# A fused attention, MoE and Fourier MLP kernel: TensorE and the load queue ordered by hand after attention

## The chip, the cores and the metric

The kernel runs on one core of a Trainium2 chip. The metric is the device time of one execution in microseconds (us), as the median of several runs. The engines are TensorE (PE in the rows; PEld is its weight load), VectorE (DVE), ScalarE (ACT), GpSimd (POOL) and SyncE (SP), which here only issues transfers.

## The reference

Three parts follow each other, on 4 batches of 544 tokens (512 local and 32 global ones) and 512 features.

1. Attention, 8 heads of 64: 32 global tokens attend to all, 512 local tokens attend to a band of 32 on each side and to the global tokens.
2. An MoE-like block: `h = relu(x @ w_in)` (512 to 1024), a 3-tap convolution along the tokens, `h * sigmoid(conv) @ w_out` back to 512.
3. A Fourier mixer and MLP: `u = x + real(fft(fft(x, tokens), features))`, normalisation of u over the features, then `u + relu(un @ w_ch1) @ w_ch2` with 2048 hidden features.

Weights arrive as float64 and are turned into float32 pairs (high and low part) on the chip; each product is three matmuls (low x high, high x low, high x high).

## The kernel before

**Attention and MoE** run together, in an order written out by hand for TensorE and the load queue (SyncE's), under `manual_schedule`: these two engines take their instructions in the order of the code, while a planner orders the others by priority. MoE goes in units u = 0 to 63: batch, half of the tokens, one of 8 blocks of hidden features. `m_g1(u)` is 12 matmuls into bank `g1`, `m_conv`, `m_tanh` and `m_gate` work on ScalarE and VectorE, and `m_g2(u - 3)` is 12 matmuls into the four banks `a0` to `a3`. When attention ends, units up to 54 have had `m_g1`; the loop from `ulast + 1` = 55 to 66 does the rest. MoE writes its result into `eo_t[b]`, three slots of the pool `up` (tag `u`) for batches 0 to 2 and one on the right side for batch 3.

**The DFT** of a batch is the generator `fft(b)`, 12 steps: a preparation on VectorE and ScalarE (L651 to L657); six first-stage pieces, for three token groups an a-piece of 8 matmuls (cosine table `c2`, and the one-row table `co`) and a b-piece of 6 (`s2`); five second-stage pieces of 9 (`c1`, `s1`). Each piece takes the next of the PSUM banks `s` and `t` in turn, and VectorE (with ScalarE) empties it. The last step stores u to `u_d[b]` in DRAM.

**The MLP** takes tokens in five chunks of 436, across batches. `load_uc(c)` reads a chunk back from `u_d` into a slot of `up`; `ln(c)` is a generator that normalises it: sums over features by matmuls with `ones` into bank `t` (mean) and `s` (variance), the centring pass L767 on VectorE, squares on ScalarE, the rest on GpSimd (chunk 0: VectorE). `cf` holds the centred chunk and keeps a slot of `up` until the end. The steps v go through `plan`, 80 pairs of chunk and hidden block: chunks 0 and 1 in two halves by turns, then 2, 3 and 4. `c_g1(v)` and `c_g2(v - 2)` are groups of 12 matmuls. The factor 1/sqrt(var) is applied when a chunk's sum is added to u.

**Weights of the MLP**: 12 blocks (`KEPT`) are unpacked during attention through the slots `r0`, `r1` and `o` of pool `stp` and parked in DRAM; `fetch_c` loads them, or raw blocks, when MoE's weight slots come free; `make_c` unpacks a raw block in two passes on ScalarE, one on GpSimd and three on VectorE (L172, L173, L202), plus ScalarE's cast. The last 16 blocks (`tail`) wait until the DFT's pool `fp` closes at step 7.

**After attention** nothing is ordered by hand. The planner places each instruction by its own forecast of when inputs are there and by the priorities of `PRIORITY`. In the order of the code, each MoE iteration has four DFT steps, first of batch 0, then (with `ln(0)` begun) of batches 1 and 2; batch 3's come two to a step in MLP steps 0 to 6; `load_uc(0)` follows the MoE loop; chunks 1 to 4 are loaded at steps 2, 25, 36 and 52.

Of the kernel before, what the change touches and what calls it, by code (L numbers as in the profile page):

```python
# [33 lines left out]
KEPT = [0, 16, 1, 17, 2, 18, 3, 19, 4, 5, 6, 7]  # L34
NT = 436
# [91 lines left out]
def fused_kernel(ctx: ExitStack, tc: tile.TileContext, d, out):  # L127
# [100 lines left out]
    right = ExitStack()  # L228
    ap1 = right.enter_context(tc.tile_pool(name="ap1", bufs=1, side="right"))
# [9 lines left out]
    stp = right.enter_context(tc.tile_pool(name="stp", bufs=1, side="right"))  # L239
# [8 lines left out]
    @prio("keep")  # L248
    def keep_load(x):
        if x is not None:  # L250
            w_raw[x] = fetch(stp, f"r{KEPT.index(x) % 2}", c_src(x))

    @prio("keep")
    def keep_make(x):
        if x is not None:
            packed[x] = put(stp, "o", unpack(mp, w_raw.pop(x), gp, True))
# [371 lines left out]
    last = ctx.enter_context(tc.tile_pool(name="last", bufs=1, side="right"))  # L628
    mag2 = last.tile([128, 512], F32, name="mag2")
# [3 lines left out]
    c2 = fp.tile([128, 2, 2, 258], F32R, name="c2")  # L633
    s2 = fp.tile([128, 2, 2, 256], F32R, name="s2")
    co = fp.tile([1, 258], F32R, name="co")
    c1 = fp.tile([92, 3, 2, NF], F32R, name="c1")
    s1 = fp.tile([92, 3, 2, NF], F32R, name="s1")
    u_t, u_d = {}, {}
# [79 lines left out]
    def c_slot(i):  # L718
        m = i % 16
        return (wp, f"w{m + (8 if i > 15 else 0)}") if m < 8 else (vp, f"v{i}")  # L720
# [16 lines left out]
    ln_t, uc_t = {}, {}  # L737
# [13 lines left out]
    def ln(c):  # L751
        n = width(c)
        ut = (uc_t[c] if c else u_t[0])[:, 0:4, 0:n]
        cf = cft[:, 0:4, 0:n]
# [8 lines left out]
        yield  # L763
        mu = bank("t")[:, 0:n]
# [12 lines left out]
        act.copy(sr[:, 0], cf[:, 0])  # L777
        dve.tensor_sub(sr[:, 1], cf[:, 0], f32(sr[:, 0]))
        yield
        yield  # L780
        va = bank("s")[:, 0:n]
        mm(va, ones, sr[:, 1], True, False)
        mm(va, ones, sr[:, 0], False, True)
        rs = uc_t[c][:, 4, 0:n]
        act.activation(rs, va, AF.Sqrt, bias=eps)
        dve.reciprocal(rs, rs)
        yield
# [22 lines left out]
    def c_g2(v):  # L810
# [15 lines left out]
        if m in last_:  # L826
            uc = uc_t[c]
            tmp = cft[:, 4, 0:n]
            for e in range(4):
                o = uc[:, e, 0:n]  # L830
                dve.tensor_mul(tmp, acc[e], uc[:, 4, 0:n])
                dve.tensor_add(o, o, tmp)
                if m == 15:
                    sp.dma_start(out[128 * e:128 * e + 128, NT * c:NT * c + n], o)

    for t, nm in ((c2, "c2"), (s2, "s2"), (c1, "c1"), (s1, "s1"), (co, "co")):
        gp.dma_start(t, d[nm])
    ffts = [fft(b) for b in range(4)]
    fq, lnq = ffts[0:1], []

    def step(queue, name):
# [7 lines left out]

    for u in range(ulast + 1, NM + LAG_G2):  # L850
        m_tanh(u - 1)
        m_g1(u, "g1")
        m_gate(u - 1)
        m_conv(u)
        m_g2(u - LAG_G2, 0)
        m_g2(u - LAG_G2, 1)
        for _ in range(4):
            step(fq, "fft")
        if not fq and not lnq:
            cft = up.tile([128, 5, NT], F32, tag="u", name="cf")  # L860
            lnq = [ln(0)]
            for _ in range(3):
                step(lnq, "ln0")
            fq = ffts[1:3]
# [5 lines left out]
    while fq:  # L870
        step(fq, "fft")
    left.close()
    lw = ctx.enter_context(tc.tile_pool(name="lw", bufs=1))
    mags += [mag2, lw.tile([128, 512], F32, name="mag1")]
    load_uc(0)
    while lnq:
        step(lnq, "ln")
    f3 = ffts[3:]
    vp = None
    tail = [x for m in range(8, 16) for x in (m, 16 + m)]  # L880
    for v in range(len(plan) + 2):
        if v < 7:
            step(f3, "f3")
            step(f3, "f3")
            if v < 4:
                make_c(20 + v)
        if v == 7:
            right.close()
            vp = ctx.enter_context(tc.tile_pool(name="vp", bufs=1, side="right"))
            for x in tail:  # L890
                fetch_c(x)
        if 8 <= v < 16:
            make_c(tail[2 * v - 16])
            make_c(tail[2 * v - 15])
# [49 lines left out]
```

## Time and profile before

| | us |
|---|---|
| median of 3 runs | 835.54 (834.47 to 838.54) |
| the profiled execution | 837.89 |
| its span, first to last instruction | 835.8 |
| TensorE busy in the span | 783.7 (94%) |
| VectorE busy | 484.1 (58%) |
| ScalarE busy | 364.0 (44%) |
| GpSimd busy | 170.0 (20%) |

The span is what the trace covers; the execution's own time has 2.1 us around it. Busy time is a sum over stages: attention fills roughly the first 334 us, MoE ends near 396, the DFTs near 477, and the MLP alone fills the rest. TensorE's granted clock is given beside the times as a share of 2.4 GHz; 0.5 is 1.2 GHz.

### The profile page before, as it was taken

Reading aid. Unit: us, or ns where it says so; the run is one execution under the profiler, and the core shown is the slowest. Engines: PE = TensorE matmul, PEld = TensorE weight load, DVE = VectorE, ACT = ScalarE, POOL = GpSimd, SP = SyncE. Lnnn points to the kernel's source line nnn. Section 1 sums busy time; section 2 is a strip of 40 time slices with the busy share of each in tenths; the row PEclk is TensorE's granted clock in tenths of the full one; section 3 lists DMA queues with packets and bytes.
Section 4 is the critical chain, followed back from the end, with each engine's and each line's share of the span. In section 5 each row is a group of like instructions: output and inputs, shape, how many; then the busy total and the mean of one; then the engine's idle time right before and its main releaser. Section 6 shows DMA issues by size and latency. Waiting matters only on the chain.

```text
span 835.8 us, 13613 instructions
## 1 busy us (share of the span) xinstructions
PE 783.7 (94%) x5272; PEld 715.1 (86%) x5272; DVE 484.1 (58%) x1162; ACT 364.0 (44%) x884; POOL 170.0 (20%) x219
## 2 busy tenths in 40 slices
PE   5769999999999999998998699999999999999996
PEld 3558888799889988997997589999999999999996
DVE  5898987668766876687726845853531232213112
ACT  5676787567666775546312156431222112111110
POOL 4544433223222321100000321111313003100000
PEclk9788999999999999999997699999999999999999
DMA  7743342344234420554022084002010011001001
GB/s 248 260 160 113 120 135 90 113 136 162 73 112 155 156 95 27 160 198 184 26 97 73 25 286 171 0 1 87 33 54 0 1 45 42 1 1 43 1 1 42
DMA packets 36896, 77.80 MB, mean 93 GB/s; under 512 B 3752, under 2 KB 22056, under 8 KB 36832
## 3 DMA queue, kind: packets, MB, share of 16 engines
q1 hardware_dynamic: 36000, 74.29, 26.0%
q0 software_dynamic: 832, 2.65, 1.3%
q8 instruction: 41, 0.67, 0.3%
q14 instruction: 23, 0.19, 0.1%
HBM read 62.11 MB, written 15.20 MB: 92 GB/s over the span
## 4 chain that ended last, share of the span: by engine, by line
PE 56%; DVE 15%; DMA 14%; ACT 10%; issue 2%; POOL 1%; SPq 1%; ACTq 0%; DVEq 0%; POOLq 0%
PE ps_a L144 25%; PE ps_g L144 14%; PE ps_pv L144 11%; DMA raw_r<-in_ch_dram 7%; PE ps_s L144 3%; ACT pb L319 3%; PE ps_t L144 2%; DMA raw_w<-in_w_in_dram 2%; DVE y L492 2%; DVE pb L307 2%; DVE y L493 2%; ACT mag L165 1%; DVE mag L173 1%; ACT y L499 1%; DMA co<-in_co_dram 1%
## 5 line engine op out<-in xcount | busy, mean ns | idle before, releaser
L144 PE MATMUL ps_g<-x,w_w 128*128 128x256 f32 (+1 forms) x768 | 113.4, 297 | 1.7 <-ACT h L481 1.7
L144 PE MATMUL ps_a<-g,w_w 128*128 128x254 f32 (+1 forms) x768 | 111.0, 292 | 0.0
L144 PEld LDWEIGHTS ps_g<-x,w_w 128*128 128x128 f32 x768 | 101.0, 190 | 11.3 <-issue 7.1
L330 POOL TENSOR_SCALAR pb<-pb,sm 128x224 f32<-128x224 f32 x128 | 82.8, 662 | 136.4 <-DVE sm L325 101.0
L144 PE MATMUL ps_a<-hd,w_w 128*128 128x436 f32 (+1 forms) x480 | 103.6, 361 | 1.2 <-ACT hd L806 1.2
L144 PEld LDWEIGHTS ps_a<-g,w_w 128*128 128x128 f32 x768 | 101.3, 189 | 0.5 <-issue 0.3
L144 PE MATMUL ps_a<-hd,w_v 128*128 128x436 f32 (+1 forms) x480 | 101.3, 361 | 0.0
L144 PEld LDWEIGHTS ps_a<-hd,w_w 128*128 128x128 f32 x480 | 89.6, 188 | 6.7 <-ACT hd L806 1.6
L144 PEld LDWEIGHTS ps_a<-hd,w_v 128*128 128x128 f32 x480 | 90.2, 188 | 5.1
L807 DVE SCALAR_TENSOR_TENSOR hd<-ps_g,hd 128x436 fp32r<-128x436 f32 (+1 forms) x40 | 24.2, 604 | 96.9 <-ACT hd L806 96.9
L807 DVE SCALAR_TENSOR_TENSOR hd<-ps_pv,hd 128x436 fp32r<-128x436 f32 (+1 forms) x40 | 24.4, 609 | 82.8 <-ACT hd L806 82.7
L166 POOL TENSOR_SCALAR mag<-mag 128x512 f32<-128x512 f32 x48 | 32.5, 678 | 181.6 <-ACT mag L165 181.1
L806 ACT ACTIVATE hd<-ps_pv 128x436 fp32r<-128x436 f32 (+1 forms) x40 | 21.3, 532 | 106.6 <-PE ps_pv L144 90.5
L806 ACT ACTIVATE hd<-ps_g 128x436 fp32r<-128x436 f32 (+1 forms) x40 | 21.3, 533 | 104.8 <-PE ps_g L144 81.6
L319 ACT ACTIVATE pb<-pb,sm 128x224 f32<-128x224 f32 x128 | 60.5, 475 | 12.9 <-DVE sm L307 12.9
L144 PE MATMUL ps_pv<-chl,w_w 128*128 128x436 f32 (+1 forms) x240 | 55.1, 377 | 6.9 <-POOL chl L769 3.5
L144 PEld LDWEIGHTS ps_pv<-chl,w_w 128*128 128x128 f32 x240 | 47.4, 199 | 10.9 <-POOL chl L769 3.8
L144 PE MATMUL ps_g<-chl,w_w 128*128 128x436 f32 (+1 forms) x240 | 52.1, 361 | 0.0
L144 PE MATMUL ps_pv<-chl,w_v 128*128 128x436 f32 (+1 forms) x240 | 50.9, 360 | 0.0
L144 PE MATMUL ps_g<-chl,w_v 128*128 128x436 f32 (+1 forms) x240 | 50.7, 360 | 0.0
L144 PE MATMUL ps_s<-qk 64*128 64x224 f32 (+1 forms) x144 | 37.5, 419 | 13.3 <-DMA qk<-in_qk_dram 4.2
L144 PEld LDWEIGHTS ps_g<-chl,w_w 128*128 128x128 f32 x240 | 44.9, 188 | 3.0 <-DVE hd L807 0.3
(203 smaller groups left out, 1397.2 us busy)
## 6 DMA issues: line engine op xcount, KB each, us to landing
v<-in_v_dram SPq DMA_DIRECT2D x16, 640.0 KB, 4.8
raw_v<-in_ch_dram SPq DMA_DIRECT2D x16, 512.0 KB, 10.8
qk<-in_qk_dram SPq DMA_DIRECT2D x16, 464.0 KB, 6.1
raw_r<-in_ch_dram SPq DMA_DIRECT2D x12, 512.0 KB, 6.4
kept<-w_o SPq DMA_DIRECT2D x12, 512.0 KB, 5.6
w_w<-kept SPq DMA_DIRECT2D x12, 512.0 KB, 3.3
qk<-in_qk_dram SPq DMA_DIRECT2D x16, 304.0 KB, 5.9
u_d<-u SPq DMA_DIRECT2D x4, 1088.0 KB, 6.4
```

Source lines behind the costliest of these rows:

```text
L144: return pe.matmul(o, a, b, start=start, stop=stop)
L165: act.activation(mag, f32(head), AF.Abs, scale=65536.0)
L166: (clamp or dve).tensor_scalar(mag, mag, TOP, 2.0, op0=ALU.min, op1=ALU.max)
L173: dve.scalar_tensor_tensor(val, head, -(2**31), val, op0=ALU.bitwise_and, op1=ALU.bitwise_or)
L307: anchor[i] = dve.tensor_tensor_reduce(out=pbs(i)[h][:, a, 0:224], in0=sb[h][:, a], in1=mask[:, 2 * where(i)[1] + a], scale=-0.125, scalar ...
L319: act.activation(p, p, AF.Exp, bias=sm[:, k:k + 1], scale=-1.0, accum_out=sm[:, 4 + k:5 + k])
L330: gp.tensor_scalar(p, p, sm[:, k:k + 1], 1.0, op0=ALU.mult, op1=ALU.mult)
L492: dve.scalar_tensor_tensor(y, hb[:, cc - 1:cc - 1 + n], convw2[:, m, 0:1], y, op0=ALU.mult, op1=ALU.add)
L493: dve.scalar_tensor_tensor(y, hb[:, cc + 1:cc + 1 + n], convw2[:, m, 2:3], y, op0=ALU.mult, op1=ALU.add)
L499: act.activation(g_t[u], g_t[u], AF.Tanh, scale=0.5)
L806: act.activation(hd[:, 0], o, AF.Relu)
L807: dve.scalar_tensor_tensor(hd[:, 1], o, 0.0, f32(hd[:, 0]), op0=ALU.max, op1=ALU.subtract)
```

## The change

From the end of attention on, TensorE and the load queue are ordered by hand as well (`manual_schedule` to the end of the kernel).

- All four DFTs form one list. `fstep` takes the next DFT step; right after the step that ends batch 1's DFT it writes chunk 1's load, after batch 2's chunk 0's load, and after batch 0's the first step of `ln(0)`. A MoE iteration has a DFT step ahead of `m_g1`, one ahead of `m_g2`'s first half, and in odd iterations one ahead of its second half: 30 of the 48 steps. MLP steps 0 to 5 have three each.
- `ln(0)` goes on in seven steps inside the MoE loop (two an iteration) and ends in MLP step 0; its 1/sqrt(var) gets a tile of its own, `rs0`. Chunk 1's `ln` begins at step 1, chunk 2's load moves from step 25 to 26, chunks 3 and 4 stay at 36 and 52. An `ln` advances by one generator step in each MLP step.
- The pool `rb` takes the place of `stp` and stays: `c2` and `s2` use the slots `r0` and `r1`, later three of the 16 late weight blocks use `r0`, `r1` and `o`. The tables are asked for in the order `c2`, `co`, `s2`, `c1`, `s1`, ahead of the other code of this stage.
- The late blocks load at step 8 in place of 7. Both `mag` buffers of the MLP lie in the pool `lw`.

```diff
+TAIL = [x for m in range(8, 16) for x in (m, 16 + m)]
...
+    rb = ctx.enter_context(tc.tile_pool(name="rb", bufs=1, side="right"))
...
-    stp = right.enter_context(tc.tile_pool(name="stp", bufs=1, side="right"))
...
-    last = ctx.enter_context(tc.tile_pool(name="last", bufs=1, side="right"))
-    mag2 = last.tile([128, 512], F32, name="mag2")
+    c2 = rb.tile([128, 2, 2, 258], F32R, tag="r0", name="c2")
+    s2 = rb.tile([128, 2, 2, 256], F32R, tag="r1", name="s2")
+    co = rb.tile([1, 258], F32R, name="co")
+    for t, nm in ((c2, "c2"), (co, "co"), (s2, "s2")):
+        gp.dma_start(t, d[nm])
...
+    for t, nm in ((c1, "c1"), (s1, "s1")):
+        gp.dma_start(t, d[nm])
+    ctx.enter_context(tc.manual_schedule(engines={mybir.EngineType.SP, mybir.EngineType.PE}))
...
-        return (wp, f"w{m + (8 if i > 15 else 0)}") if m < 8 else (vp, f"v{i}")
+        if m < 8:
+            return (wp, f"w{m + (8 if i > 15 else 0)}")
+        k = TAIL.index(i) - 13
+        return (vp, f"v{i}") if k < 0 else (rb, ("r0", "r1", "o")[k])
...
         yield
         yield
+        if c == 0:
+            yield
         mu = bank("t")[:, 0:n]
...
-        rs = uc_t[c][:, 4, 0:n]
+        rs = rs_t[c] = uc_t[c][:, 4, 0:n] if c else rs0
...
-    for t, nm in ((c2, "c2"), (s2, "s2"), (c1, "c1"), (s1, "s1"), (co, "co")):
-        gp.dma_start(t, d[nm])
-    ffts = [fft(b) for b in range(4)]
-    fq, lnq = ffts[0:1], []
+    fq = [fft(b) for b in range(4)]
+    lnq = []
...
+    def fstep(n=1):
+        for _ in range(n):
+            step(fq, "fft")
+            for c, b in ((1, 1), (0, 2)):
+                if b in u_d and c not in uc_t:
+                    load_uc(c)
+            if 0 in u_d and not lnq and not ln_t:
+                lnq.append(ln(0))
+                step(lnq)
+
+    early = 7
+
     for u in range(ulast + 1, NM + LAG_G2):
+        fstep()
         m_tanh(u - 1)
         m_g1(u, "g1")
         m_gate(u - 1)
         m_conv(u)
+        if lnq and early:
+            early -= 1
+            step(lnq)
+        fstep()
         m_g2(u - LAG_G2, 0)
+        if u % 2:
+            fstep()
         m_g2(u - LAG_G2, 1)
-        for _ in range(4):
-            step(fq, "fft")
...
+        if lnq and early:
+            early -= 1
+            step(lnq)
...
-    load_uc(0)
-    while lnq:
-        step(lnq, "ln")
-    f3 = ffts[3:]
...
     for v in range(len(plan) + 2):
-        if v < 7:
-            step(f3, "f3")
-            step(f3, "f3")
+        if v < 8:
+            for _ in range(3):
+                fstep()
             if v < 4:
                 make_c(20 + v)
-        if v == 7:
+        if v == 8:
+            while fq:
+                fstep()
             right.close()
...
+        while v == 0 and lnq:
+            step(lnq)
-        if v in (2, 25, 36, 52):
-            c = {2: 1, 25: 2, 36: 3, 52: 4}[v]
-            load_uc(c)
+        if v in (1, 26, 36, 52):
+            c = {1: 1, 26: 2, 36: 3, 52: 4}[v]
+            if c > 1:
+                load_uc(c)
             lnq.append(ln(c))
-        step(lnq, "ln")
+        step(lnq)
         c_g1(v)
         c_g2(v - 2)
```

## Rows read from the trace of the kernel before

**Rows 1.** The page, granted TensorE clock in 40 slices, tenths of full speed.
```profile
PEclk9788999999999999999997699999999999999999
```

**Rows 2.** Windows: stretch, length, busy PE, PEld, DVE, ACT, POOL (count), clock, DMA share, GB/s.
```profile
337.10:388.80 51.70, 48.48 (x362) 45.94 (x360) 37.98 (x78) 25.64 (x59) 1.06 (x3) 1.00 0.64 214
388.80:392.10 3.30, 2.80 (x8) 2.58 (x9) 3.21 (x7) 2.63 (x3) 0.00 (x0) 0.50 0.03 5
392.10:450.30 58.20, 56.97 (x334) 52.27 (x333) 30.47 (x61) 14.04 (x30) 2.32 (x3) 1.00 0.12 44
450.30:470.70 20.40, 17.58 (x70) 13.97 (x69) 15.97 (x25) 5.01 (x10) 3.40 (x2) 0.50 0.32 99
470.70:477.50 6.80, 5.24 (x33) 3.65 (x32) 6.15 (x12) 1.65 (x1) 0.87 (x1) 1.00 0.00 0
477.50:484.30 6.80, 3.62 (x10) 3.34 (x11) 4.34 (x2) 1.66 (x1) 5.03 (x2) 0.50 0.18 70
484.30:494.00 9.70, 8.46 (x42) 7.35 (x40) 1.88 (x4) 3.28 (x6) 1.87 (x3) 1.00 0.83 272
494.00:828.80 334.80, 334.80 (x1691) 317.22 (x1690) 119.57 (x174) 79.64 (x131) 41.89 (x30) 1.00 0.11 39
```

**Rows 3.** Waits of TensorE, 337 to 500 us: total, times, longest.
```profile
PE ps_pv L144 <- POOL chl L769: 3.5, 1, 3.5
```

**Rows 4.** Timeline of TensorE: start, length, instruction, tiles, count.
```profile
342.02 0.28 PE L144 MATMUL ps_t<-s,fl 128*92 128x256 f32 x1
...
342.73 1.77 PE L144 MATMUL ps_g<-x,w_w 128*128 128x292 f32 x12
...
349.89 0.28 PE L144 MATMUL ps_s<-c,fl 128*92 128x258 f32 x1
...
351.10 0.50 PE L144 MATMUL ps_a<-g,w_w 128*128 128x254 f32 x2
...
360.25 1.31 PE L144 MATMUL ps_s<-c,ab 92*128 92x274 f32 x9
...
503.23 2.55 PE L144 MATMUL ps_g<-chl,w_w 128*128 128x436 f32 x12
```

**Rows 5.** Timeline of VectorE: first and last pass preparing the first DFT.
```profile
334.25 0.72 DVE L651 TENSOR_TENSOR ff<-u 128x548 f32<-128x548 f32 x1
...
338.64 0.73 DVE L657 TENSOR_TENSOR fl<-ff,fh 128x548 fp32r<-128x548 f32 x1 [0.32 <-ACT fh L656]
```

**Rows 6.** Groups of VectorE's instructions by line, 374 to 530 us.
```profile
L786 DVE RECIPROCAL uc<-uc 128x436 f32<-128x436 f32 x2 | 5.8, 2876 | 1.5 <-ACT uc L785 1.5
...
L704 DVE TENSOR_TENSOR u<-u 128x544 f32<-128x544 f32 x6 | 4.3, 718 | 0.0
...
L202 DVE TENSOR_TENSOR w_w<-mag,w_w 128x512 fp32r<-128x512 f32 x4 | 2.7, 687 | 0.1
...
L767 DVE TENSOR_TENSOR cf<-u,ps_t 128x1744 f32<-128x1744 f32 x1 | 2.0, 1959 | 0.0
L689 DVE SCALAR_TENSOR_TENSOR u<-u,ps_t 128x273 f32<-128x273 f32 x4 | 1.8, 438 | 4.7 <-PE ps_t L144 4.7
```

**Rows 7.** Timelines of three engines between chunk 0's last group and chunk 2's mean.
```profile
567.45 5.36 PE L144 MATMUL ps_a<-hd,w_v 128*128 128x436 f32 x26
...
573.24 0.61 DVE L832 TENSOR_TENSOR uc<-uc,cf 128x436 f32<-128x436 f32 x1
...
581.41 2.09 POOL L758 TENSOR_TENSOR cf<-uc 128x872 f32<-128x872 f32 x1 [21.48 <-DMA uc<-u_d]
...
585.33 0.61 DVE L761 TENSOR_TENSOR chl<-cf,chl 128x436 fp32r<-128x436 f32 x1 [1.37 <-ACT chl L760]
```

**Rows 8.** Timelines of GpSimd and VectorE in chunk 1's normalisation.
```profile
476.63 3.99 POOL L769 TENSOR_TENSOR chl<-cf,chl 128x1744 fp32r<-128x1744 f32 x1 [13.00 <-ACT chl L768]
...
477.38 3.82 DVE L703 TENSOR_TENSOR u<-u 128x544 f32<-128x544 f32 x1
```

**Rows 9.** DMA issues by tile: KB each, median us to landing.
```profile
u_d<-u SPq DMA_DIRECT2D x4, 1088.0 KB, 6.4
```

More of the change, by code (lines that the diff above doesn't have):

```diff
@@ L250, in keep_load @@
         if x is not None:
-            w_raw[x] = fetch(stp, f"r{KEPT.index(x) % 2}", c_src(x))
+            w_raw[x] = fetch(rb, f"r{KEPT.index(x) % 2}", c_src(x))
     @prio("keep")
@@ L255, in keep_make @@
         if x is not None:
-            packed[x] = put(stp, "o", unpack(mp, w_raw.pop(x), gp, True))
+            packed[x] = put(rb, "o", unpack(mp, w_raw.pop(x), gp, True))
     @prio("keep")
@@ L735, in make_c @@
         (ch2 if i > 15 else ch1)[i % 16] = t
-    ln_t, uc_t = {}, {}
+    ln_t, uc_t, rs_t, cft = {}, {}, {}, []
     def width(c):
@@ L753, in ln @@
         ut = (uc_t[c] if c else u_t[0])[:, 0:4, 0:n]
-        cf = cft[:, 0:4, 0:n]
+        if c == 0:
+            cft.append(up.tile([128, 5, NT], F32, tag="u", name="cf"))
+        cf = cft[0][:, 0:4, 0:n]
         chl = xp.tile([128, 10, NT], F32R, tag="x", name="chl")
@@ L763, in ln @@
         yield
+        if c == 0:
+            yield
         mu = bank("t")[:, 0:n]
@@ L827, in c_g2 @@
             uc = uc_t[c]
-            tmp = cft[:, 4, 0:n]
+            tmp = cft[0][:, 4, 0:n]
             for e in range(4):
                 o = uc[:, e, 0:n]
-                dve.tensor_mul(tmp, acc[e], uc[:, 4, 0:n])
+                dve.tensor_mul(tmp, acc[e], rs_t[c])
                 dve.tensor_add(o, o, tmp)
@@ L834, in c_g2, with step @@
                     sp.dma_start(out[128 * e:128 * e + 128, NT * c:NT * c + n], o)
-    for t, nm in ((c2, "c2"), (s2, "s2"), (c1, "c1"), (s1, "s1"), (co, "co")):
-        gp.dma_start(t, d[nm])
-    ffts = [fft(b) for b in range(4)]
-    fq, lnq = ffts[0:1], []
-    def step(queue, name):
+    fq = [fft(b) for b in range(4)]
+    lnq = []
+    def step(queue, name="ln"):
         while queue:
@@ L854, in fused_kernel @@
         m_conv(u)
+        if lnq and early:
+            early -= 1
+            step(lnq)
+        fstep()
         m_g2(u - LAG_G2, 0)
+        if u % 2:
+            fstep()
         m_g2(u - LAG_G2, 1)
-        for _ in range(4):
-            step(fq, "fft")
[L859 to L864, printed above, removed]
+        if lnq and early:
+            early -= 1
+            step(lnq)
         k = u - (NM - 8)
@@ L869, in fused_kernel @@
             fetch_c(16 + k - 3)
-    while fq:
-        step(fq, "fft")
     left.close()
     lw = ctx.enter_context(tc.tile_pool(name="lw", bufs=1))
-    mags += [mag2, lw.tile([128, 512], F32, name="mag1")]
-    load_uc(0)
-    while lnq:
-        step(lnq, "ln")
-    f3 = ffts[3:]
+    mags += [lw.tile([128, 512], F32, name=f"mag{i}") for i in range(2)]
+    rs0 = lw.tile([128, NT], F32, name="rs0")
     vp = None
-    tail = [x for m in range(8, 16) for x in (m, 16 + m)]
     for v in range(len(plan) + 2):
-        if v < 7:
-            step(f3, "f3")
-            step(f3, "f3")
+        if v < 8:
+            for _ in range(3):
+                fstep()
             if v < 4:
                 make_c(20 + v)
-        if v == 7:
+        if v == 8:
+            while fq:
+                fstep()
             right.close()
             vp = ctx.enter_context(tc.tile_pool(name="vp", bufs=1, side="right"))
-            for x in tail:
+            for x in TAIL:
                 fetch_c(x)
         if 8 <= v < 16:
-            make_c(tail[2 * v - 16])
-            make_c(tail[2 * v - 15])
-        if v in (2, 25, 36, 52):
-            c = {2: 1, 25: 2, 36: 3, 52: 4}[v]
-            load_uc(c)
+            make_c(TAIL[2 * v - 16])
+            make_c(TAIL[2 * v - 15])
+        while v == 0 and lnq:
[4 more added lines that the diff above has]
+                load_uc(c)
             lnq.append(ln(c))
-        step(lnq, "ln")
+        step(lnq)
         c_g1(v)
```

3 lines of the change are left out of this document (removed).

## Prediction

> **What bounds the kernel now.** I read the page first: in 40 slices TensorE is nearly always busy, and its granted clock is full but for one place past the middle [rows 1]. So TensorE sets the end, and the question is how much of its time is not work. The windows view, cut where the clock changes, answers it for the part that the change touches, from the end of attention's last hand-ordered matmul (337.1 us) to TensorE's last matmul (828.8 us) [rows 2]. Two things are to be seen. Busy time is 477.95 of 491.7 us, so TensorE stands idle for 13.75 us, all before 494. And three stretches run at the lower of the two clock levels, 1.2 GHz: 2.80, 17.58 and 3.62 us of busy time that would take half at 2.4 GHz; that is 12.0 us. Together 25.75 us can be won. After 494 nothing is idle and the clock is full: there the change can only lose. Third I read who ends the idle time: the longest single wait is 3.5 us for GpSimd's part of chunk 1's normalisation [rows 3]; the rest is spread over the tail of the DFTs and normalisations.
>
> A count by work checks this. A 12-matmul MLP group takes 2.38 us (its row says 2.55, of which some 0.16 lies over the next row, as in each run of matmuls here), so 80 MLP steps of two groups take 380.4 us. A DFT is three a-pieces of 1.2 us, three b-pieces of 0.71 and five second-stage pieces of 1.15: 11.5 us, 46 for four. The MoE's remaining 21 groups of 12 take 1.4 to 1.6 us, 32.9 in all; 20 statistics matmuls take 0.2 each, 4.0 [rows 4]. The sum is 463.3 us against 491.7 passed: 28.4 us lost. So some 2.7 us more sit in seams between pieces, inside what is shown as busy.
>
> **What the change removes.** The half-clock stretch at 450 to 471 is the end of the third DFT and the whole fourth, packed together with little else, each piece waiting for VectorE. Spread in threes over MLP steps 0 to 5 this packing is gone. Loading chunk 1 behind the second DFT, while MoE still runs, moves its landing far ahead of step 8 where its result is used; that removes the 3.5 us wait and the half clock after it. The constants are asked for earlier and the one-row table no longer comes last. I credit all 25.75 us and half of the seams, 27 us, and subtract what the fixed order costs. Without any such cost the gain would be 28.4.
>
> **What the fixed order costs.** TensorE now takes its instructions as written: a matmul whose input is late holds every matmul behind it, where the planner of before put another group first. The load queue likewise. Term by term:
>
> 1. *The mean of chunk 2.* Its slot comes free only when chunk 0's results have been stored; the load is now written at step 26 and the mean matmul at the head of step 28, two steps (2 x 4.76 = 9.5 us) after the last group of chunk 0. In the trace that group starts at 567.45 and so ends at 569.8. VectorE adds the last quarter until 573.9, it is stored and the new chunk loaded, GpSimd starts on it at 581.41, and VectorE finishes the mean's input at 585.94: 16.2 us after the group [rows 7]. None of this chain is changed. So TensorE stands for 16.2 - 9.5 = 6.7 us with nothing to put in front. Before, the planner put the mean later, and TensorE had no idle time there at all [rows 2]. After such a pause the clock is at 1.2 GHz: after the 3.18 us idle in the window 477.5 to 484.3, 3.62 us of dense work ran at half, which is 1.8 us lost. Together 8.5 us; bounds 6 (store and load 1 us quicker, no clock) and 10.5. Chunks 3 and 4 have four steps, 19.0 us, between the same events, 16.2 needed: nothing.
>
> 2. *The opening of the MLP.* Steps 0 and 1 have six DFT pieces of the third DFT and one MLP group each: 6.45 + 0.4 + 4.76 = 11.6 us of TensorE. Then comes the fourth DFT's first piece, which needs all of its preparation. VectorE must do, from the end of MoE: pieces 7.7 us (0.42 to 0.86 each, and twice the pair of 0.72), two weights' conversions of three 0.69 passes (4.2), two hidden passes (1.2) and the preparation (3.3): 16.4 us [rows 6]. The reciprocal of 2.88 us can wait. So the piece is some 4.8 us late. The preparation alone took 334.25 to 339.37, 5.1 us, over two engines [rows 5]; it fits if VectorE is free. I take 5 us; bounds 1 (the planner puts preparation ahead of the conversions) and 9 (the reciprocal goes first, and a clock dip follows).
>
> 3. *Banks in the later DFT steps.* Pieces go by turns through two PSUM banks, back to back in threes, and chunk 1's mean falls on the bank just filled by the third piece of step 3: about 1 us there, and a few tenths for each of the other threes. 2 us; bounds 1 and 4.
>
> 4. *Normalising chunk 0 inside MoE.* The mean uses a bank that the next DFT piece but one needs, at the head of MoE iteration 61, and VectorE's centring pass takes 1.96 us [rows 6]. VectorE was busy for 37.98 of the 51.7 us from 337.1 to 388.8 [rows 2], with MoE, one DFT and a part of the second; now nearly all of two DFTs and this normalisation (about 8 us) go through it in some 60 us, so it will often be late. I take 3.5 us; bounds 1.5 and 6. Before, the same stretch held 3.22 + 0.50 us of idle time, which is in the 25.75.
>
> 5. *Loads behind chunk 1.* On the load queue chunk 1 waits for the second DFT's store (1,088 KB, 6.4 us to land [rows 9]), and three raw weights stand behind it, some 10 us later than written. They are used from step 7 on; ScalarE may stand for one of them. 1 us; bounds 0 and 4.
>
> The wait that heads the preparation of the first DFT stays: it starts when attention's buffers go, at 334.25 in both, and the first piece comes at 338.5, its one-row matmuls at 339.2, against 339.37 ready. That is 0.2 us, within term 4's bounds. Steps 8 to 25 and 29 to 81 are the same matmuls in the same order as the dense part of before; their weights load from about step 6, ten steps before use. The tail is unchanged.
>
> Sum: 8.5 + 5 + 2 + 3.5 + 1 = 20.0 lost, 27 won: 7 us net, about 0.9%. The profiled execution took 837.89 us (span 835.8, 2.1 around it), 2.35 above the median; I put the gain on the median: 835.5 - 7 = 828.5, rounded to 828.
>
> **The rivals.**
>
> *VectorE keeps up* (0.2). Terms 2 to 5 at their low bounds, 3.5 us, and term 1 at 7: 27 + 1.4 - 10.5 = 17.9, about 818. For it: from 392.1 to 450.3, with MLP groups and DFT pieces mixed, TensorE was idle for only 1.23 of 58.2 us and VectorE busy for 30.47 [rows 2]. Against it: it needs conversions and preparation in the right order on VectorE, which is left to the planner.
>
> *GpSimd holds VectorE* (0.15). GpSimd normalises chunk 1 in steps 1 to 5, just when VectorE empties the DFT banks. The trace shows the price: while GpSimd's 3.99 us subtraction ran until 480.62, VectorE's addition of two SBUF tiles, elsewhere 0.72 us, took 3.82 and ended at 481.2 [rows 8]. Then the bank behind it is late. With the additions (2.09, and half of that for the half-wide one, both twice [rows 7]) GpSimd has some 10 us of such work in those steps; if half of it holds VectorE in front of a bank, 5 us more than forecast: 833, no measurable change. It decides where a bank's emptying stands behind such an addition. The Trainium skill, SBUF — State Buffer, in "Who interferes with whom", has the rule: the two engines share a pair of ports, held for the whole instruction, and a vector instruction with two SBUF inputs waits fully against a GpSimd read. The trace agrees (3.82 against 0.72). By the rule alone, with each of those 10 us in VectorE's way, the result would be 838.
>
> *The clock stays low at the MLP's opening* (0.15): slower than before. Steps 0 to 4 are 34 us of full-speed work; each microsecond of it that runs at 1.2 GHz adds one. If the late pieces of term 2 drop the clock at step 1 and it stays low for half of these steps, 17 us are added: about 845. It decides once more than 7 + 4 = 11 us of full-speed work runs at half. For it: 450.3 to 470.7 stayed low for 20.4 us, with 17.58 busy. Against it: there were DFT pieces and waits alone, and where dense groups of 12 follow, the clock was full again after 3.3 and 6.8 us, idle time included [rows 2]; every step here has such a group.
>
> **How the numbers follow.** Forecast 0.5, the fast rival 0.2, the two slow ones 0.15 each. About 0.5% (4.2 us) is what a measurement can tell from no change. Its own range, with any two terms at the same bound, is 822 to 835. Faster by over 0.5% (below 831.4): 0.43 of the forecast's 0.5, all of the fast rival, a little of GpSimd's: 0.65. Slower (above 839.7): the clock rival, 0.15. The same: 0.20. The range 815 to 840 leaves out the clock rival and an edge of the fast one.
>
> **What would show it.** In the new profile: no half-clock stretch of 20 us near the end of the DFTs; DFT pieces between MLP groups until step 5; no wait for chunk 1 at step 8; one TensorE wait of 6 to 7 us on the mean of chunk 2 near 560, with about 3 us at half clock behind it; waits of several us at the fourth DFT's first piece; 1 to 3 us on VectorE's centring of chunk 0 inside MoE. I am wrong if the wait at chunk 2 is missing (the gain is then 8.5 us greater), or if TensorE's idle time before step 6 is well above 11 us.

## The result: 0.6% slower

The changed kernel takes 841.1 us in the median of 20 runs (836.1 to 844.7), the kernel before 835.6 us in the 20 runs beside it; the ratio is 1.006 (95% interval 1.0039 to 1.008). The forecast was 828 us, 13 less.

The profiled execution of the changed kernel took 836.21 us (span 834.4). That is one of its two quickest, 4.9 us under its median. In part its attention ended early: the first matmul behind it starts at 329.36 us, and at 332.1 in the mean of the fourteen other traces of this document (328.2 to 334.6). So the two traces are compared over the part that the change orders, from the first matmul after attention's last to the start of the last pass over the accumulators: 497.3 us before (334.06 to 831.35), 500.6 after (329.36 to 829.92). That is 3.3 us more, where the medians differ by 5.5; the other 2.2 us these two traces do not show. All lines of the changed kernel stand one to eleven lines lower.

The page, the granted clock in 40 slices; it answers to [rows 1]:

```profile
PEclk9899999999999999999899999997999999999999
```

The dip of two slices past the middle (439 to 481 us) is gone; two smaller ones stand in its place, near 415 and 570 us. The low slice at the start lies in attention, as three did before. The windows view says what they are (stretch, length, busy PE, PEld, DVE, ACT, POOL, clock, DMA share, GB/s), answering to [rows 2]:

```profile
329.36:369.50 40.14, 36.98 (x282) 34.41 (x278) 32.53 (x70) 19.63 (x46) 1.22 (x3) 1.00 0.48 149
369.50:373.80 4.30, 4.30 (x22) 4.13 (x22) 2.31 (x2) 2.53 (x4) 0.00 (x0) 0.61 0.09 23
373.80:411.00 37.20, 34.77 (x248) 32.07 (x247) 29.62 (x57) 18.13 (x39) 5.21 (x4) 1.00 0.54 181
411.00:419.00 8.00, 5.55 (x21) 4.48 (x22) 8.00 (x18) 1.84 (x3) 1.82 (x1) 0.57 0.00 0
419.00:472.00 53.00, 52.04 (x291) 48.12 (x290) 29.69 (x50) 22.71 (x39) 11.10 (x8) 1.00 0.49 170
472.00:480.00 8.00, 5.31 (x26) 4.36 (x25) 7.96 (x15) 6.23 (x12) 1.62 (x2) 1.00 0.88 316
480.00:562.30 82.30, 80.89 (x404) 75.20 (x402) 40.73 (x66) 22.21 (x40) 7.58 (x10) 1.00 0.05 16
562.30:576.00 13.70, 6.95 (x22) 6.35 (x22) 3.19 (x3) 2.74 (x3) 5.08 (x3) 0.63 0.12 41
576.00:829.92 253.92, 250.89 (x1265) 236.85 (x1263) 63.77 (x91) 39.99 (x64) 25.89 (x13) 1.00 0.06 20
```

TensorE is busy for 477.7 of 500.6 us: 22.9 us idle, against 16.3 before over the same part (481.0 busy of 497.3). In both some 2.5 us of this are the tail, VectorE's last passes behind the last matmul. The lower clock costs 4.30 x 0.39 + 5.55 x 0.43 + 6.95 x 0.37 = 6.6 us, against 12.0 [rows 2]. So the pauses grew by 6.6 us, the clock gave back 5.4, and what is left, 2.1 us, lies in seams within the busy time. The waits say where the pauses lie (waiting matmul, releaser, total us, times, longest):

```profile
PE ps_t L145 <- DVE chl L770: 7.7, 2, 6.7
PE ps_s L145 <- DVE u L696: 4.8, 1, 4.8
PE ps_a L145 <- DVE cf L842: 4.8, 5, 1.4
PE ps_t L145 <- DVE cf L778: 2.1, 1, 2.1
PE ps_t L145 <- DVE ab L675: 0.9, 1, 0.9
```

Every one is VectorE; none is a load. They sum to 20.3 us; the rest of the 22.9 is the tail. The matmuls around them, from TensorE's timeline (start, length, tiles, count; in brackets the idle time ahead and what ended it):

```profile
365.83 0.66 PE L145 MATMUL ps_t<-chl,ones 128*128 128x436 f32 x2 [0.97 <-DVE chl L770]
368.56 0.36 PE L145 MATMUL ps_t<-c,fl 128*92 128x258 f32 x1 [2.06 <-DVE cf L778]
...
413.45 2.22 PE L145 MATMUL ps_s<-c,ab 92*1 92x274 f32 x9 [4.84 <-DVE u L696]
415.46 3.79 PE L145 MATMUL ps_g<-chl,w_w 128*128 128x436 f32 x12
...
476.03 0.86 PE L145 MATMUL ps_a<-hd,w_w 128*128 128x436 f32 x3 [1.31 <-DVE cf L842]
478.28 0.86 PE L145 MATMUL ps_a<-hd,w_w 128*128 128x436 f32 x3 [1.39 <-DVE cf L842]
...
569.11 1.10 PE L145 MATMUL ps_t<-chl,ones 128*128 128x436 f32 x2 [6.75 <-DVE chl L770]
570.00 4.57 PE L145 MATMUL ps_pv<-chl,w_v 128*128 128x436 f32 x12
```

Four places: chunk 0's mean inside MoE (366 to 374); the opening of the MLP (408 to 419); the changes of accumulators where a half of a chunk ends (476 and 517, and 0.67 us at 606), which the prediction does not have; chunk 2's mean (569). Behind the first, a MoE group of 12 takes 2.83 us in place of 1.77 (at 369.84); behind the second and the fourth, MLP groups of 12 take 3.79 and 4.57 in place of 2.55. VectorE's timeline, ahead of the second and third place:

```profile
408.17 2.86 DVE L797 RECIPROCAL rs<-rs 128x436 f32<-128x436 f32 x1
410.96 0.54 DVE L770 TENSOR_TENSOR chl<-cf,chl 128x436 fp32r<-128x436 f32 x1
411.42 0.67 DVE L174 SCALAR_TENSOR_TENSOR mag<-raw_w,mag 128x512 int32<-128x512 int32 x1
412.02 0.59 DVE L818 SCALAR_TENSOR_TENSOR hd<-ps_pv,hd 128x436 fp32r<-128x436 f32 x1
412.54 0.42 DVE L693 SCALAR_TENSOR_TENSOR u<-u,ps_s 128x273 f32<-128x273 f32 x1
412.89 0.42 DVE L696 SCALAR_TENSOR_TENSOR u<-u,ps_s 128x271 f32<-128x271 f32 x1
...
473.09 0.59 DVE L842 TENSOR_TENSOR cf<-ps_a,rs 128x436 f32<-128x436 f32 x1
473.61 0.67 DVE L174 SCALAR_TENSOR_TENSOR mag<-raw_v,mag 128x512 int32<-128x512 int32 x1
474.21 0.60 DVE L843 TENSOR_TENSOR uc<-uc,cf 128x436 f32<-128x436 f32 x1
474.85 0.61 DVE L818 SCALAR_TENSOR_TENSOR hd<-ps_pv,hd 128x436 fp32r<-128x436 f32 x1
475.38 0.60 DVE L842 TENSOR_TENSOR cf<-ps_a,rs 128x436 f32<-128x436 f32 x1
```

The bank that the third DFT's last piece needs is emptied (L693, L696) behind a reciprocal of 2.86 us that nothing asks for soon, and behind passes of a conversion (L173 at 407.21, and L174). And between two passes that empty accumulators (L842) stand a conversion of a late weight, an addition and a hidden pass: 2.3 us from one to the next, while TensorE fills a bank in 0.6.

### The profile page after: what moved, and what is told of

It is laid out like the page before. It is cut to its first block, busy times and chain, and to the rows that moved or that the text cites. A ratio compares the mean times of both kernels' runs of the same rounds, so it can differ in the third digit from the quotient of the medians.

```text
span 834.4 us, 13622 instructions
## 1 busy us (share of the span) xinstructions
PE 778.8 (93%) x5272; PEld 710.4 (85%) x5272; DVE 477.1 (57%) x1162; ACT 364.5 (44%) x884; POOL 173.7 (21%) x219
## 4 chain that ended last, share of the span: by engine, by line
PE 54%; DVE 19%; DMA 14%; ACT 8%; issue 2%; SPq 2%; POOL 0%; DVEq 0%; ACTq 0%; POOLq 0%
PE ps_a L145 24%; PE ps_g L145 13%; PE ps_pv L145 11%; DMA raw_r<-in_ch_dram 9%; PE ps_s L145 4%; PE ps_t L145 3%; ACT pb L320 2%; DVE pb L308 2%; DVE y L493 2%; DMA raw_w<-in_w_in_dram 2%; DVE y L494 2%; DVE mag L174 2%; DVE mag L173 1%; DMA raw_v<-in_ch_dram 1%; ACT mag L166 1%
## 5 line engine op out<-in xcount | busy, mean ns | idle before, releaser
L331 POOL TENSOR_SCALAR pb<-pb,sm 128x224 f32<-128x224 f32 x128 | 84.5, 676 | 127.9 <-DVE sm L326 81.5
L145 PE MATMUL ps_a<-hd,w_v 128*128 128x436 f32 (+1 forms) x360 | 77.4, 362 | 1.4 <-DVE cf L842 1.4
L145 PEld LDWEIGHTS ps_a<-hd,w_v 128*128 128x128 f32 x360 | 67.8, 189 | 6.3 <-DVE cf L842 2.5
L817 ACT ACTIVATE hd<-ps_pv 128x436 fp32r<-128x436 f32 (+1 forms) x40 | 21.3, 533 | 117.5 <-PE ps_pv L145 117.4
L167 POOL TENSOR_SCALAR mag<-mag 128x512 f32<-128x512 f32 x48 | 35.3, 736 | 113.3 <-ACT mag L166 112.7
L145 PE MATMUL ps_pv<-chl,w_v 128*128 128x436 f32 (+1 forms) x240 | 52.9, 370 | 0.0
L767 POOL TENSOR_TENSOR cf<-uc 128x872 f32<-128x872 f32 (+1 forms) x4 | 8.3, 2068 | 212.5 <-DMA uc<-u_d 143.0
L145 PE MATMUL ps_pv<-chl,w_w 128*128 128x436 f32 (+1 forms) x240 | 50.8, 360 | 0.0
L145 PEld LDWEIGHTS ps_pv<-chl,w_v 128*128 128x128 f32 x240 | 46.8, 195 | 2.8
```

The source lines that it names most:

```text
L145: return pe.matmul(o, a, b, start=start, stop=stop)
L167: (clamp or dve).tensor_scalar(mag, mag, TOP, 2.0, op0=ALU.min, op1=ALU.max)
L331: gp.tensor_scalar(p, p, sm[:, k:k + 1], 1.0, op0=ALU.mult, op1=ALU.mult)
L817: act.activation(hd[:, 0], o, AF.Relu)
```

## The experiments

The kernel before was run again beside each group of experiments. Its median lay between 834.4 and 837.2 us, so the ratios to it (with their 95% intervals) are compared; the changed kernel has 1.006.

**The mean of chunk 2, two steps later.** One wait alone. An `ln` advances by one `yield` in each MLP step, so two more move the mean from step 28 to 30.

```diff
-        if c == 0:
+        for _ in range({0: 1, 2: 2}.get(c, 0)):
             yield
```

> The changed kernel, with the mean of chunk 2 written two steps later (step 30 in place of 28). Theory (the fixed order's waits make the slowdown): the single wait of 6.75 us on chunk 2's mean and the half clock after it, about 9.5 us together, go; 841.1 becomes about 831.5, ratio to the kernel before 0.995, and the trace has no wait there. Rival (the chain only moves its stall): step 32 then waits for chunk 2's normalised tokens, as mean to use is now 9.5 us against some 8.5 needed; the time stays within 2 us of 841.

833.3 us, ratio 0.9958 (0.9929 to 0.9987): 1.0% less than the changed kernel. The wait on chunk 2's mean is gone and no new one took its place, though the accumulators' waits near 480 are now followed by half clock. Term 1 of the prediction is confirmed: from the last DFT piece to the end the part takes 376.6 us in place of 384.3, 7.7 less.

**The opening and the accumulators, one at a time.** First the reciprocal of chunk 0 behind step 5's hidden pass (`behind` fixes an order between two instructions):

```diff
-        dve.reciprocal(rs, rs)
+        if c:
+            dve.reciprocal(rs, rs)
...
+        if v == 5:
+            behind(dve.reciprocal(rs0, rs0), hd_ins[5])
```

> The changed kernel, with the 2.9 us reciprocal of chunk 0 held back on VectorE behind step 5's last hidden pass. Theory: the 4.8 us wait for a bank in step 1 comes from this one pass in front of the bank's emptying; the wait and the half clock behind it (2.4 us) go, 841.1 becomes about 834, ratio 0.998. Rival (VectorE is simply overloaded there, 16.4 us of work before the fourth DFT's first piece against 11.6 us of TensorE): the wait moves to the next step's first DFT piece and at most 2 us are won, 839.

840.5 us, 1.0045 (1.0025 to 1.0065). The wait of 4.84 us falls to 2.43 and no further, since two passes of a conversion are still ahead of the emptying; the accumulators' waits grow from 4.8 to 6.1 us. The 0.15% won is within the intervals, so nothing is shown to be won by this edit alone.

Then the conversions of 14 late weights behind the emptying of chunk 0's accumulators (`emptied[7]` is the last pass that does it):

```diff
-        if 8 <= v < 16:
-            make_c(TAIL[2 * v - 16])
-            make_c(TAIL[2 * v - 15])
+        if v == 8:
+            make_c(TAIL[0])
+            make_c(TAIL[1])
+        if 10 <= v < 17:
+            make_c(TAIL[2 * v - 18], emptied[7])
+            make_c(TAIL[2 * v - 17], emptied[7])
```

> The changed kernel, with 14 of the 16 late weights' conversions held back on VectorE until the accumulators of chunk 0's first half are emptied. Theory: three of the five accumulator waits (together 4.8 us) come from conversions between the emptying passes; those at the end of chunk 0's first half (2.7 us and their seams) go, those at chunk 1's half (1.4 us) stay: 841.1 becomes about 838, ratio 1.003. Rival: the conversions, now 5 us later, meet the end of chunk 1's half and give as much back; 841.

840.4 us, 1.004 (1.0021 to 1.0059): 0.2% less, within the intervals too. The accumulators of chunk 0's first half are waited for no longer; at the end of chunk 1's half, into which the conversions were pushed, the waits grow. TensorE's timeline there has one of 2.50 us where the changed kernel has 0.97 and 0.43, and the group of 12 behind it takes 3.93 us in place of 2.55 (granted clock 0.63 from 520.9 to 525.5):

```profile
520.93 1.05 PE L145 MATMUL ps_a<-hd,w_v 128*128 128x436 f32 x3 [2.50 <-DVE cf L850]
521.78 3.93 PE L145 MATMUL ps_g<-chl,w_v 128*128 128x436 f32 x12
```

Last, chunk 0's mean in the bank `pv`, which no DFT piece needs (and the other means stay in `t`):

```diff
-        mu = bank("t")[:, 0:n]
+        mu = bank("t" if c else "pv")[:, 0:n]
```

> The changed kernel, with the mean of chunk 0 in the bank of the MLP's groups, idle during MoE, in place of the DFT's bank. Theory: the 2.1 us wait of the next DFT piece for VectorE's centring pass goes, and with it the half clock that follows (1.9 us): 841.1 becomes about 837.5, ratio 1.002. Rival: VectorE is late with the MoE's own passes there, and the piece or the group behind it waits as long; 841.

836.9 us, 1.000 (0.9978 to 1.0022): 0.6% won, term 4. The wait of 2.06 us and the half clock at 369 to 374 are gone. In the trace the part up to the last DFT piece takes 113.7 us in place of 116.3, but the part behind it 386.3 in place of 384.3: a half-clock stretch is new there, near 480. So the 0.6% is read from the medians, and the trace shows only a part of it.

**Four and five edits together.** The four edits above (the mean again two steps later, the reciprocal again behind step 5's hidden pass, which the first expectation words otherwise), and then three early conversions moved as well:

```diff
-            if v < 4:
-                make_c(20 + v)
+            if v == 0:
+                make_c(20)
+            if 2 <= v < 5:
+                make_c(19 + v, hd_ins[1])
```

> Four edits together on the changed kernel: the mean of chunk 2 one step later, the reciprocal of chunk 0 behind the first MoE gating passes, the later late-weight conversions behind the emptying of chunk 0's accumulators, and the mean of chunks 1 and 2 in the bank of t with chunk 0's in the bank of pv. Theory (four separate in-order waits, each with a clock stretch of its own): the single ratios were 0.9958, 1.0045, 1.004 and 1.000 against 1.006, so the gains are 1.0, 0.15, 0.2 and 0.6 per cent; they add to about 2 per cent, so 0.986 (824 us), idle time from the end of attention to the last accumulator down from 22.9 to 12 us or less. Rival (what is won on one wait comes back at the next, as VectorE's work in these steps is the bound and the clock falls at whichever wait is left): no better than the mean alone, 0.993 to 0.997, with the idle time at 16 us or more.

> The four edits of the kernel before, and the conversions of three more late weights moved from MLP's first four steps to behind its second hidden tile, so that VectorE empties the banks of the fourth DFT first. Theory (VectorE's order at the opening of MLP makes the wait of 4.84 us on the emptied bank and the half clock behind it): that wait goes below 1.5 us, the clock is not at half between 411 and 420, and the time falls by 3 to 5 us against the four edits alone, ratio about 0.982. Rival (VectorE has more work in these steps than TensorE lasts, in whatever order): same as the four edits alone within 0.2 per cent, with an equal wait a few steps later.

821.9 us, 0.9855 (0.9824 to 0.9886), and 820.3 us, 0.9844 (0.981 to 0.9879). The four single gains (1.0, 0.15, 0.2, 0.6) add to 1.95%, and together they bring 2.05: these waits are separate, and mending them turns the loss into a gain. The fifth edit brings 0.1% more, within the intervals, where 3 to 5 us were expected: the wait that it aims at is still 1.9 us, against 2.5 without it, though the clock no longer falls there. In both a wait of 2.5 us on the accumulators at chunk 1's half remains, with half clock for some 3.5 us behind it.

**Who orders.** The same code with the order by hand for neither engine (the line left out), for the load queue alone (the diff), and for TensorE alone (`PE` in that place):

```diff
-    ctx.enter_context(tc.manual_schedule(engines={mybir.EngineType.SP, mybir.EngineType.PE}))
+    ctx.enter_context(tc.manual_schedule(engines={mybir.EngineType.SP}))
```

> The changed kernel without the hand-written issue order after attention: its emission, its buffers and its load instructions stay, but the planner chooses the order of both TensorE and the load queue again. Theory (the loss lies in the fixed order, in which one late operand stops all that stands behind it): the planner takes other work into the waits on the mean of chunk 2 and on the accumulators, and the kernel comes back to within 0.5 per cent of the one before, 0.995 to 1.003. Rival (the loss lies in the rest of the edit, the moved emission and the loads behind chunk 1): 1.006 or more.

> The changed kernel with the hand-written order kept for the load queue alone; the planner orders TensorE after attention. Theory (no load is waited for in the changed kernel, so the load queue's order is worth nothing either way): the same as the kernel in which the planner orders both, within 0.3 per cent. Rival (the order of the loads matters, since the planner's TensorE order asks for other weights earlier): over 0.5 per cent slower than that kernel, with waits on DMAs in TensorE's or VectorE's idle time.

> The changed kernel with only TensorE's order by hand; the planner orders the load queue. Theory (TensorE's fixed order alone costs what the changed kernel loses against the planner's orders, 2.5 to 2.9 per cent, and the load queue's order is worth nothing to it): 1.003 to 1.009, the same waits. Rival (the two orders by hand lose together, because a load stands behind another): below 1.000.

817.7 us, 0.9808 (0.9776 to 0.984) with the planner for both; 815.7 us, 0.9777 (0.9745 to 0.9809) with the loads by hand; 843.0 us, 1.007 (1.0051 to 1.009) with TensorE by hand. The theory of the first expectation was too timid, and its rival is refuted: the rest of the edit is no loss but a gain of about 2%. The order by hand of TensorE, and it alone, turns that into a loss; it costs 2.6% with the planner's loads and 2.8% with those by hand. The load queue's order by hand is worth 0.3% and 0.1%, both within the intervals.

**By hand to step 8 only.** There the last DFT is over and the dense part begins:

```diff
-    ctx.enter_context(tc.manual_schedule(...))
+    hand = ExitStack()
+    hand.enter_context(tc.manual_schedule(...))
...
         if v == 8:
             while fq:
                 fstep()
+            hand.close()
```

> The changed kernel with both orders by hand only up to MLP step 8, where the last DFT is over; from there on the planner orders both. What is left of the loss is then that of MoE, the DFTs and the opening of the MLP; what goes is the wait on the mean of chunk 2 and those on the accumulators at the ends of the chunk halves. Theory (the loss against the planner's order, 2.5 to 2.9 per cent, is in both parts: 1.0 per cent at the mean, as taking it one step later showed, 0.3 to 0.5 at the accumulators): 0.991 to 0.996. Rival (the late part is the whole loss, and the DFTs by hand are as good as by the planner): 0.983 or below; or nothing but the mean is won: 0.996 or above.

823.1 us, 0.9831 (0.9813 to 0.9849): well below the theory's 0.991, and at the edge of the rival that had the late part as the whole loss. Some 2.3 of the 2.8% lie behind step 8. The windows, split at the last DFT piece, of the changed kernel, of the one with the mean late, and of this one:

```profile
329.36:445.65 116.29, 107.28 (x721) 98.56 (x718) 86.88 (x170) 51.84 (x105) 16.70 (x12) 0.96 0.39 128
445.65:829.92 384.27, 370.39 (x1849) 347.43 (x1847) 130.91 (x197) 84.17 (x139) 42.81 (x31) 0.99 0.12 43
```

```profile
333.19:450.65 117.46, 108.25 (x721) 99.21 (x718) 87.35 (x170) 51.87 (x105) 16.76 (x12) 0.94 0.39 126
450.65:827.23 376.58, 369.16 (x1849) 346.27 (x1847) 131.31 (x198) 83.40 (x139) 43.15 (x31) 1.00 0.13 44
```

```profile
331.91:449.39 117.48, 108.55 (x722) 99.62 (x719) 86.93 (x169) 52.43 (x106) 16.47 (x12) 0.94 0.41 135
449.39:817.09 367.70, 365.16 (x1849) 345.65 (x1847) 131.66 (x198) 82.55 (x137) 43.05 (x32) 1.00 0.12 40
```

The same 1,849 matmuls take 384.3, 376.6 and 367.7 us. The mean is 7.7 of the 16.6 us. The other 8.9 lie in the main at the accumulators: the only waits of TensorE left behind the last DFT piece in the kernel with the mean late are five on them, 5.0 us together, and in the one by hand to step 8 there is none. What the planner does there is seen in its TensorE timeline:

```profile
477.08 0.96 PE L145 MATMUL ps_a<-hd,w_w 128*128 128x436 f32 x4
477.88 1.96 PE L145 MATMUL ps_g<-chl,w_w 128*128 128x436 f32 x9
479.67 0.75 PE L145 MATMUL ps_a<-hd,w_w 128*128 128x436 f32 x3
480.26 0.75 PE L145 MATMUL ps_g<-chl,w_w 128*128 128x436 f32 x3
```

Three matmuls fill one accumulator and a fourth begins the next; then part of the next hidden tile's group (bank `g`) runs while VectorE empties the others. The kernel before does the same, as its timeline at the end of chunk 1's half shows, without a wait:

```profile
529.38 0.96 PE L144 MATMUL ps_a<-hd,w_v 128*128 128x436 f32 x4
530.18 2.54 PE L144 MATMUL ps_g<-chl,w_v 128*128 128x436 f32 x12
532.56 2.14 PE L144 MATMUL ps_a<-hd,w_v 128*128 128x436 f32 x10
```

In the order by hand all four accumulators follow each other and the group of `g` comes behind them, so TensorE waits two times at 476 and two times at 517. In the same way the planner puts chunk 2's mean behind three matmuls of the next group, at 570.57, with no wait.

**By hand to step 8, mended.** The same, with three of the edits in the part by hand: the bank, the reciprocal, the early conversions.

> Both orders by hand up to MLP step 8 and by the planner from there on, as in the kernel with ratio 0.9831, and in the part by hand three of the edits that were tried before: the mean of chunk 0 in the bank of pv, the reciprocal of chunk 0 late, the conversions of three late weights behind the second hidden tile. Theory (the fixed order of the DFT part is no loss in itself; it loses where VectorE is late, and there alone): the first part, to the last DFT piece, takes 107 to 110 us in place of 117.5, the second stays at about 368, together 475 to 478; ratio 0.973 to 0.978, as good as the planner's order for TensorE throughout (0.9777) or a little better. Rival (a fixed order gives each gain back at the next late operand): 0.981 or above.

816.3 us, 0.976 (0.9736 to 0.9785), the lowest ratio of all, on a par with the planner's order for TensorE throughout (0.9777). Its windows, split in the same way:

```profile
334.60:442.48 107.88, 103.26 (x722) 95.60 (x718) 84.20 (x168) 52.46 (x106) 15.91 (x12) 1.00 0.45 147
442.48:810.17 367.69, 365.15 (x1849) 345.62 (x1847) 134.11 (x199) 82.29 (x137) 43.02 (x32) 1.00 0.12 40
```

Full clock in both, 7.2 us idle in all. The DFT part takes 107.9 us in place of 117.5. So its fixed order, threes included, is no measurable loss in itself; it loses where VectorE comes late.

**Where the gain of the rest comes from.** Two halves of it, both under the planner: the kernel with the loads by hand, but chunk 1 loaded late; and the kernel before, with chunk 1 loaded early and nothing else.

```diff
-            for c, b in ((1, 1), (0, 2)):
-                if b in u_d and c not in uc_t:
-                    load_uc(c)
+            if 2 in u_d and 0 not in uc_t:
+                load_uc(0)
...
-            if c > 1:
-                load_uc(c)
+            load_uc(c)
```

> The kernel with the load queue by hand and TensorE by the planner (ratio 0.9777), with one thing undone: chunk 1 is loaded at MLP step 1, as late as its normalisation asks for it, in place of behind the second DFT. Theory (the 18 us that this kernel gains on the one before come from chunk 1's early load: it gives the planner MLP groups to put between the pieces of the fourth DFT): most of it is lost, 0.990 to 1.000, with a wait on chunk 1's normalisation and a half-clock stretch of 10 us or more around 450 to 480, as before. Rival (they come from the DFT steps being spread over MoE and MLP steps): within 0.4 per cent of 0.9777, no new wait.

```diff
-        rs = uc_t[c][:, 4, 0:n]
+        rs = rs_t[c] = uc_t[c][:, 4, 0:n] if c else rs0
...
-    load_uc(0)
+    load_uc(1)
...
-            load_uc(c)
+            load_uc(c if c > 1 else 0)
```

> The kernel before, all by the planner, with one thing added: chunk 1 is loaded in chunk 0's place, behind the MoE loop, and chunk 0 in chunk 1's place at step 2 (1/sqrt(var) of chunk 0 has a tile of its own for that). No order by hand, no spreading, no moved tables. Theory (the early chunk 1 is the gain): 0.978 to 0.988, the half-clock stretch of 20 us at 450 to 471 is gone or much shorter, since groups of chunk 1 stand between the pieces of the fourth DFT. Rival (the spreading is the gain): within 0.4 per cent of 1.

826.9 us, 0.9873 (0.9855 to 0.9891), between the two expectations: the late load takes back 1.0 of 2.2%. And 834.8 us, 0.9981 (0.9962 to 1.0), the rival: the early load alone is worth next to nothing. The traces show why. With the load late, TensorE's timeline has one wait of 5.45 us on chunk 1's mean, and the clock is at half from about 455.5 to 472.5, much as in the kernel before [rows 2]. With the load early in the kernel before, GpSimd starts on chunk 1 at 431, but the planner's order has its mean at 467, behind most of the fourth DFT. The rows, one of the former, then GpSimd's and TensorE's of the latter:

```profile
461.41 1.09 PE L145 MATMUL ps_t<-chl,ones 128*128 128x436 f32 x2 [5.45 <-DVE chl L770]
```

```profile
431.21 2.10 POOL L758 TENSOR_TENSOR cf<-uc 128x872 f32<-128x872 f32 x1 [28.63 <-DMA uc<-u_d]
```

```profile
467.16 0.93 PE L144 MATMUL ps_t<-chl,ones 128*128 128x436 f32 x2
```

So the early load pays only with the rest of the edit, and the rest, the spread DFT and the tables asked for earlier, is the larger part (1.3%). These two were not taken apart.

## Why the prediction was wrong

Over the ordered part the mended kernel (by hand to step 8, three edits) takes 475.6 us, 21.7 less than the kernel before and 25.0 less than the changed one. It still has 7.2 us of idle time: 2.5 are the tail, which the prediction's 25.75 leave out, and 4.6 lie ahead of the last DFT piece, nearly all on waits that terms 2 to 4 are about (2.0 us on the third DFT's bank, 1.2 at chunk 1's mean, 1.0 at chunk 0's). With these 4.6 us counted as a cost of the fixed order, 26.3 us were there to win, and 29.6 were lost again; the prediction had 27 won and 20 lost. So the credit was near, and the cost was 9.6 us too low. That is 10.3 of the 13 us. Another 0.5 is the rounding of 828.5, and 2.2 the medians' difference that the two traces do not show.

*The step that failed* is the sentence "Steps 8 to 25 and 29 to 81 are the same matmuls in the same order as the dense part of before", which put the changes of accumulators at nothing. They are the same matmuls, but not in the same order: where a half of a chunk ends, the planner lets a group of the next hidden tile run between the four accumulators, and the code has them in a row. The prediction had seen that before had no idle time behind 494 [rows 2] and took it for the work's nature; it was the planner's doing. Behind step 8 it charged 8.5 us, all term 1; the runs show 16.6, of which 8.9 are not the mean. Between the kernel with the mean late and the one by hand to step 8, 4.9 of these are idle time (7.4 against 2.5), all of it the accumulators' waits, and 1.2 half clock behind them (3.6 us of work at 0.66 from 483 to 488). Of the remaining 2.8 about 1 is the three matmuls right behind each wait (0.86 us in place of 0.6); the rest no view resolves. Without these 8.9 us the result would have been a gain of some 3 us, by an estimate from the medians (841.1 - 8.9 against 835.6).

*The size of the credit* is not shown as closely: it is 26.3 us only if all that the mended kernel still waits for is the fixed order's doing. If the 4.6 us could not be won in any order, it is 21.7.

The terms ahead of step 8 (2 to 5) come to 13.0 us so counted, of which the mended kernel's first part takes back 8.4 (116.3 to 107.9); predicted were 11.5. That is close, but in part by luck, since not every place was the one named:

1. *Term 1, the mean of chunk 2*: right. 6.75 us idle, predicted 6.7, and about 2.6 of half clock, predicted 1.8; taken away by itself it gave 7.7 us, predicted 8.5.
2. *Term 2, the opening*: the place and a step of it wrong, the size near. Not the fourth DFT's first piece is late but the third's last, for its bank: 4.84 us, and 2.4 us of half clock behind it, 7.2 against 5. So the size is luck. "The reciprocal of 2.88 us can wait" was true and did not help, since the planner put it first; that was in the bounds.
3. *Term 3, banks*: 0.92 us at chunk 1's mean, at the lower bound.
4. *Term 4, chunk 0 inside MoE*: 0.97 and 2.06 idle and 1.7 of half clock, 4.7 against 3.5, within the bounds; the 2.06 us are at the bank and the pass that were named, the 0.97 are the mean's own input.
5. *Term 5, loads*: nothing, the lower bound; no wait of TensorE ends on a load.

Neither of the two signs of being wrong came: the wait at chunk 2 is there, and TensorE's idle time up to the last DFT piece is 9.0 us, below the 11 named. Neither looks at the changes of accumulators, where the miss was.

The rivals: VectorE did not keep up, the waits are all on it. The low clock at the opening cost 2.4 us, where that rival decides above 11; the kernel came out slower, but not by its cause. GpSimd did hold VectorE, but little. The rows of both engines in chunk 1's normalisation:

```profile
404.07 1.53 DVE L658 TENSOR_TENSOR ff<-u 128x548 f32<-128x548 f32 x1
405.53 1.13 DVE L707 TENSOR_TENSOR u<-u 128x544 f32<-128x544 f32 x1
```

```profile
403.90 1.11 POOL L768 TENSOR_TENSOR cf<-cf 128x436 f32<-128x436 f32 x1
404.99 1.09 POOL L167 TENSOR_SCALAR mag<-mag 128x512 f32<-128x512 f32 x1
```

The two VectorE passes take 0.72 us elsewhere [rows 5, 6], so 1.2 us were lost where the rival had 5. VectorE has no idle time from there to the emptying at 412.54, so these 1.2 us are in the wait of 4.84. Each ends some 0.6 us after the GpSimd pass beside it, at 405.60 and 406.66 against 405.01 and 406.08. That is what the Trainium skill, SBUF — State Buffer, "Who interferes with whom", leads one to expect: a vector instruction with two SBUF inputs contends with a GpSimd instruction that reads SBUF, since the shared ports are locked. The trace agrees, and it stays a small term here.

## What to carry to other kernels

A dense stretch without idle time in a planner's order says nothing about the same work in an order written out: look at what the planner puts between two users of one bank, at every change of accumulators, before calling that stretch unchanged. Fix an order only where VectorE's order is fixed with it, or give a late operand more slack, as two steps more did for chunk 2's mean: the same code lost 0.6% with every wait in place and won 2.4% with three waits mended and the dense part left to the planner. And try an edit's restructuring and its fixed order apart: here one was worth 2% and the other cost nearly 3.

## What the runs showed of the hardware

The length of a pause alone does not tell whether the clock drops. At the end of chunk 0's half the changed kernel pauses for 1.31 and 1.39 us (its rows at 476.03 and 478.28 above), and the clock stays full: 1.00 from 474 to 484. The kernel with chunk 0's mean in `pv` pauses there for 0.72 and 1.72 us, and the matmuls behind the second pause run at half clock (0.66 in the mean from 474 to 484), three of them in 1.46 us in place of 0.86. A longer pause, 1.89 us ahead of 405.44 in the kernel with five edits, is followed by full clock (1.00 from 404 to 408). The rows of the second kernel:

```profile
474.90 0.86 PE L145 MATMUL ps_a<-hd,w_w 128*128 128x436 f32 x3 [0.72 <-DVE cf L842]
477.47 1.46 PE L145 MATMUL ps_a<-hd,w_w 128*128 128x436 f32 x3 [1.72 <-DVE cf L842]
```

In this kernel the half clock at 369 to 374 had gone and this one was new, 100 us later. What decides which pause drops the clock stays open here; that such stretches come and go with small shifts makes a single edit's gain hard to forecast. A matmul in front holds all that stand behind it: in the 6.75 us ahead of 569.11 no other ran, though the group behind it needs no part of chunk 2; with the mean two steps later it ran without a wait. The Trainium skill, PSUM — Partial Sum Buffer, "Engine vs sequencer instructions", has it that matmuls start in program order; the trace agrees, and the planner's orders are fixed in the same way, as its own wait of 5.45 us on chunk 1's mean shows.
